# Longer row-half stretches in a fused attention and token-mixing kernel

## The chip, the cores and the metric

The kernel runs on one core of a Trainium2 chip. The metric is the device time of the program in microseconds, the median of several runs.

## The reference

The output mixes an attention with a token-mixing MLP through a sigmoid gate per token, in float32. Sizes: 2048 tokens (S), width 640 (D), 32 query heads of width 20 that share one key and one value head, hidden width 1728 (F).

```python
g = sigmoid((x * gate_w).sum(-1, keepdims=True))
# attention
q = (x @ wq) -> (32 heads, S, 20);  k = x @ wk;  v = x @ wv
p = softmax(q @ k.T * 20 ** -0.5);  a = (p @ v, heads joined) @ wo
# MLP over the token axis
h = layernorm(x)
u = gelu(einsum("bsd,sf->bdf", h, w1) + b1)
b = transpose(einsum("bdf,fs->bds", u, w2) + b2)
out = g * a + (1 - g) * b
```

## The kernel before

Large products are kept accurate by splitting each float32 operand into a high and a low part (tiles named `hi` and `lo`) and adding three products. The order of the instructions on every engine is written out by hand; no scheduler moves them.

A first part makes the projections q, k, v, the layer norm h and the first 10 of the 28 tiles of the MLP's first product. What follows is the loop that the change is about. It goes through 512 **units**: 32 groups n (512 queries of four heads) times 16 key blocks kb of 128 keys. For each unit:

- four **score** matmuls `s` (`qk`, L632), each with 62 rows of contraction, so each uses only one half of TensorE's rows, half 0 or half 1 (two matmuls per half). Both halves can run at once. ScalarE turns each into a `p` tile by an exponential (L635).
- one **o visit** (`pv_mm`, L659): p times v, accumulated over the 16 key blocks. It uses all rows and a quarter of the columns for each of the four heads, so it cannot run beside the row-half work.
- two extra rows of the score contraction hold minus the row maximum, which a separate pass has to find beforehand: **max matmuls** `ms` (L466, 60 rows, also in row halves), each read by a VectorE reduction (L469) into a tile `mp`. 64 of them make the maxima of one group; `ms_done` then reduces them (mm, L480) and splits them on GpSimd (mn, L482 to L484). `store_max` transposes them on VectorE (mt, L490) and stores them to memory, and `fetch_max` (L498) brings them into the query tile `qst` of a later group. The max pass runs 48 matmuls per half ahead of the scores when the loop starts.

Into the row half that the scores leave idle goes other matrix work, in steps `g` of 64 rows by 320 columns: first the rest of the MLP's first product (**W1**, L867), then its second product (**W2**, L704), then the attention's **output product** (L816) for the first half of the tokens. The weights of W1 and W2 arrive in chunks: a load (L99, L105), then a split on GpSimd (L123, L124) in `w1_upto`. A g accumulator is one PSUM bank, which both row halves must not write at once; so whenever the half changes, VectorE writes a `flag` (L645) after the last g step of one half, and the first of the other half waits for it.

One **phase** k of the loop, with b = k % 2: half b runs the four score matmuls of units k-1 and k and three or four ms; the other half runs g steps and the rest of the ms; then unit k-1 gets its o visit. `beside` merges the two halves' lists into one program order by nominal costs (`X_US` 0.232 for s and ms, `F_US` 0.147 for g). The last 24 units (`stretch`, the **tail**) take two units together, with two o visits behind them. PSUM has eight banks: three for s, three for ms, one for g, one for o.

Behind group n's last visit o is transposed on VectorE (ot, L668), divided by the row sums on GpSimd, transposed back (on, L675) and split into oh and ol, which are stored (`later`, one step per phase through `settle`). The tanh chain of the gelu goes through `pop_chain`, one step per phase. All loads and stores are issued by SyncE's queue in program order.

Of the kernel before, what the change touches and what calls it, by code (L numbers as in the profile page):

```python
# [17 lines left out]
P = 128  # L18
S, D, H, DH, F = 2048, 640, 32, 20, 1728
NS = S // P  # L20
# [17 lines left out]
def mix_kernel(ctx: ExitStack, tc: tile.TileContext, A_x, A_wq, A_wk, A_wv, A_wo,  # L38
# [400 lines left out]
    u0 = upool.tile([P, 2 * FC * HD2], F32R, name="u0")  # L439
    u_hi = [view(t, 0, FC) for t in (u0, slot[0])]  # L440
    u_lo = [view(t, FC * HD2, FC) for t in (u0, slot[0])]
    pp_pool = ctx.enter_context(tc.tile_pool(name="pp", bufs=12))
    ev = ctx.enter_context(tc.tile_pool(name="ev", bufs=1))
    ps_m = ctx.enter_context(tc.tile_pool(name="ps_m", bufs=3, space=PSUM))
    ps_g = ctx.enter_context(tc.tile_pool(name="ps_g", bufs=1, space=PSUM))
    mpool = ctx.enter_context(tc.tile_pool(name="mpool", bufs=2))
    mmpool = ctx.enter_context(tc.tile_pool(name="mmpool", bufs=2))

    row_max = {}
    mtiles = {}  # L450
    given = [0, 0]
    issued = [0, 0]
# [23 lines left out]
    def ms_done():  # L476
        n = len(row_max)
        if n < NU and min(issued) >= 32 * (n + 1):
# [5 lines left out]
            nc.gpsimd.tensor_sub(mn[:, 1, :], mm, f32(mn[:, 0, :]))  # L484
            row_max[n] = mn

    def store_max(n):
        mn = row_max[n]
        mt = mpool.tile([P, 32], F32, name="mt")
        nc.vector.transpose(mt, f32(mn).rearrange("p j c -> p (j c)"))  # L490
        nc.sync.dma_start(out=m_scr[n], in_=mt)
# [110 lines left out]
    def second():  # L602
        right.close()
        pools["rows"] = ctx.enter_context(tc.tile_pool(name="rows", bufs=3, side="right"))

    wos = {}

# [45 lines left out]
    def pv_mm(u):  # L653
        n, kb = units[u]
        if kb == 0:
            otile[0] = ps_o.tile([P, NB], F32, name="o")
        o = otile[0]
        for hh in range(4):
            nc.tensor.matmul(o[32 * hh:32 * hh + 32, :], v_sb[:, kb, :], ptiles.pop((u, hh)),  # L659
                             start=(kb == 0), stop=(kb == NS - 1), skip_group_check=True)  # L660
        if kb == NS - 1:
            qb, g = divmod(n, NQ)
            ot = ev.tile([P, NB // 32, 32], F32, name="ot")
            rl = ev.tile([P, NB // 32], F32, name="rl")
            on = ev.tile([P, NB], F32, name="on")
            oh = ev.tile([P, NB], F32R, name="oh")
            ol = ev.tile([P, NB], F32R, name="ol")
            nc.vector.transpose(ot.rearrange("p c e -> p (c e)"), o)  # L668

            def scale():  # L670
                nc.vector.reciprocal(rl, ot[:, :, DH])
                (nc.vector if spare[0] else nc.gpsimd).tensor_mul(ot, ot, rl[:, :, None].to_broadcast([P, NB // 32, 32]))

            def back():
                nc.vector.transpose(on, ot.rearrange("p c e -> p (c e)"))  # L675

            def high():
                osplit[:] = [oh, ol]
                if n < NU - 1:
                    nc.gpsimd.tensor_copy(oh, on)  # L680
                else:
                    nc.scalar.activation(oh, on, AF.Copy)

            def low():
                (nc.vector if n == NU - 1 else nc.gpsimd).tensor_sub(ol, on, f32(oh))
                for j, t in enumerate((oh, ol) if n < NU - 1 else ()):
                    for hh in range(4):
                        r = (4 * g + hh) * DH
                        nc.sync.dma_start(out=o_scr[j, r:r + DH, qb * NB:(qb + 1) * NB],
                                          in_=f32(t[32 * hh:32 * hh + DH, :]))  # L690

            later.extend((None, scale, back, high, low))

    def b2_jobs(st):
        hold = {}

        def mm(fc, k, d, half):
            if not hold.get("n"):
                hold["p"], hold["n"] = ps_g.tile([P, NB], F32, name="g"), 0
            wh, wl = w1t[W2 + 4 * st + fc // HS]  # L700
            w, u = ((wh, u_hi), (wh, u_lo), (wl, u_hi))[k]
            hold["n"] += 1
            r = slice(64 * half, 64 * half + 64)
            other_tile(half, nc.tensor.matmul(hold["p"][:, :HD2], w[r, fc % HS, :], u[d][r, fc, :],  # L704
                             start=(hold["n"] == 1), stop=(hold["n"] == 6 * FC - 3)))
# [10 lines left out]

        def steps(d):
            full = [[(fc, k), (fc, k)] for fc in range(FC - 1) for k in range(3)]
            return [[lambda fc=fc, k=k, h=h: mm(fc, k, d, h) for h, (fc, k) in enumerate(f)]
                    for f in full + [[(FC - 1, 0), (FC - 1, 1)], [(FC - 1, 2)]]]  # L720

        return (lambda: None), [(steps(d), lambda d=d: done(d)) for d in range(2)]

# [129 lines left out]
    def b1_jobs(d, fc):  # L853
# [16 lines left out]
        def done():  # L870
            gelu(d, fc, [hold["p"]])

        return load, [([[lambda h=h, st=st, k=k: mm(st, k, h) for h in range(2)]
                        for st in range(NS) for k in range(3)], done)]

    def batches(tiles, counts):
# [10 lines left out]
                    out.append(([r[c[j]:c[j + 1]] for r, c in zip(rows, cut)], rest, [done] if j == cnt - 1 else []))  # L887
        return out

    k_tail = len(units) - TAIL  # L890
    todo = [divmod(i, FC) for i in range(PRO, 2 * FC)]
    seq = batches([b1_jobs(*t) for t in todo], [5] * len(todo))
    for i, (steps, rest, done) in enumerate(seq):
        item, j = divmod(i + 1, 5)
        rest.insert(0, lambda c=4 * (PRO + item) + (48 * j // 5) // 12: w1_upto(c + 4))
    b2 = [b2_jobs(st) for st in range(NS)]
    m = len(seq)
    seq += batches(b2, [4] * 2 * NS)
    for st in range(NS - 1):
        for j, n in ((1, 1), (2, 2), (3, 4)):  # L900
            seq[m + 8 * st + 4 + j][1].append(lambda c=W2 + 4 * (st + 1) + n: w1_upto(c))
    seq[-1][1].append(second)
    for c in range(DC):
        seq[m + 9 + 8 * c][1].append(lambda c=c: load_wo(c))
        seq[m + 11 + 8 * c][1].append(lambda c=c: split_wo(c))
    aj = [a_jobs(st) for st in range(NS - 8)]
    seq[-8][1].append(aj[0][0])
    twice = k_tail // 2 - len(seq) - 2 * len(aj)
    seq += batches(aj, [2 if i < twice else 1 for i in range(2 * len(aj))])
    ph = [(rows[1 - b], rest if b else [], done if b else []) for rows, rest, done in seq for b in range(2)]  # L910
    assert len(ph) == k_tail
    for i, k in enumerate((443, 451, 459, 467, 473, 477, 481, 485)):
        ph[k][1].append(lambda i=i: tail_load(i))

    X_US, F_US = 0.232, 0.147

    def beside(rows0, rows64, x):
        lanes = [list(rows0), list(rows64)]
# [20 lines left out]
        if not (r0 and st in held):  # L939
            tail_job(i)  # L940
    w1_upto(4 * PRO + 4)
    def settle(k):
        for _ in range(2 if spare[0] else 1):
            f = later.pop(0) if later else None
            if f:
                f()
        pop_chain()

    def visit(u):
        pv_mm(u)  # L950
        n, kb = units[u]
        if kb == 7 and n + 1 < NU:
            store_max(n + 1)
        if kb == 9 and n + 1 < NU:
            fetch_max(n + 1)

    for k in range(k_tail):
        b = k % 2
        ss = [lambda u=u, pr=pr: qk(u, pr, b) for u in (k - 1, k) for pr in range(2) if u >= 0]
        fs, rest, done = ph[k]  # L960
        ms = [[f for f in (ms_next(x) for _ in range(c)) if f] for x, c in (((b, 3), (1 - b, 1)) if len(fs) < 12 else ((b, 4), (1 - b, 0)))]
        lanes = [None, None]
        lanes[b] = lane_x(ss, ms[0])
        lanes[1 - b] = lane_f(ms[1], fs, done)
        if k == 0:
            (m0, m1, m2), (s0, s1) = ms[0], ss
            lanes[0] = [(3 * X_US, m0), (3 * X_US, m1), (X_US, s0), (X_US, m2), (X_US, s1)]
        beside(*lanes, b)
        ms_done()
        spare[0] = len(row_max) == NU  # L970
        settle(k)
        for f in rest:
            f()
        if k == k_tail - 4:
            raw = last_wo()
        if k == k_tail - 2:
            w_last = split_last(raw)
        if k:
            visit(k - 1)

    def stretch(k, n):
        lanes = [None, None]
        for b in range(2):
            own = [j for j in range(k, k + n) if j % 2 == b]
            ss = [lambda u=u, pr=pr, b=b: qk(u, pr, b) for j in own for u in (j - 1, j) for pr in range(2) if u < len(units)]
            fs = tail_take(b, math.ceil(len(tail[b]) * n / (len(units) + 1 - k)) + (n == 1) * (3 if not ss else -3))
            cut = [0] + [round(len(fs) * x) for x in ((0.25, 0.5, 0.75, 1.0) if n == 1 else
                                                          (0.18, 0.53, 0.82, 1.0) if b == k % 2 else (0.41, 0.71, 1.0, 1.0))]
            lanes[b] = [x for i in range(4) for x in [(X_US, y) for y in ss[i:i + 1]] +
                        [(F_US, f) for f in fs[cut[i]:cut[i + 1]]]]  # L990
        beside(*lanes, None)
        for j in range(k, k + n):
            settle(j)
            if 13 <= j - k_tail < 17:
                tail_load(8 + j - k_tail - 13)
            visit(j - 1)

    stretch(k_tail, 1)
    for k in range(k_tail + 1, len(units), 2):
        stretch(k, 2)  # L1000
    accs = {}

    for c in range(CUT // P, DC):
# [57 lines left out]
```

## Time and profile before

| | us |
|---|---|
| median of three runs (1698.72 to 1698.84) | 1698.8 |
| the profiled execution, its span | 1697.4 |
| loop: first W1 step to the end of the last single visit | 179.4 to 1614.5 |
| busy in the span: PE, DVE, ACT, POOL | 1690.2, 1435.0, 1189.8, 570.4 |

The profile shows one execution. PE is the matrix engine, PEld its weight loads, DVE VectorE, ACT ScalarE, POOL GpSimd, SPq SyncE's queue of transfers. A row of the order of time has the start and the duration in us, the engine, the source line, the operation, output and input with their sizes, a count, and in brackets the idle time before it with what ended it. A row of a group has a count, busy time in us and the mean of one in ns. A row of the waits has the time in all, how many and the longest. Matmuls overlap, so a PE that is busy 100% is not a PE at its peak.

### The profile page before, as it was taken

What the parts mean: (1) busy time and instruction counts of PE and PEld (TensorE: products, weight loads), DVE (VectorE), ACT (ScalarE), POOL (GpSimd) and SP (SyncE); (2) the same over time, 40 slices, a digit from 0 to 9 for tenths busy, and PEclk for the clock granted to TensorE, in tenths of its full rate; (3) what the DMA queues carried; (4) which work ended last, traced back from release to release, by engine and by line L of the source; (5) the groups of instructions that cost most, each with busy time, mean ns of one, the idle gap of its engine ahead of it and who ended that gap; (6) DMA issues with size and microseconds to landing.
All of it is one profiled execution on the core that took longest, in us unless ns stands there. A gap on an engine that the chain in (4) does not pass through costs nothing.

```text
span 1697.4 us, 39056 instructions
## 1 busy us (share of the span) xinstructions
PE 1690.2 (100%) x14865; PEld 1103.0 (65%) x14865; DVE 1435.0 (85%) x2915; ACT 1189.8 (70%) x2322; POOL 570.4 (34%) x723
## 2 busy tenths in 40 slices
PE   9999999999999999999999999999999999999998
PEld 7899766666666666666666666666666666555666
DVE  6679898888888888888888888888888888888734
ACT  4445677777777777777777777777777777777775
POOL 6467644544445454322222212222221111111200
PEclk9999999999999999999999999999999999999999
DMA  7665322222222222121112222212111222344411
GB/s 212 192 177 147 94 64 69 65 64 64 60 69 70 70 70 69 50 64 52 57 49 70 70 60 62 63 56 61 52 52 35 62 63 64 92 113 144 132 57 57
DMA packets 173377, 135.45 MB, mean 80 GB/s; under 512 B 32729, under 2 KB 139382, under 8 KB 173190
## 3 DMA queue, kind: packets, MB, share of 16 engines
q1 hardware_dynamic: 172902, 132.63, 28.0%
q8 instruction: 117, 1.92, 0.5%
q14 instruction: 70, 0.57, 0.1%
q10 hardware_dynamic: 288, 0.33, 0.1%
HBM read 100.27 MB, written 31.65 MB: 78 GB/s over the span
## 4 chain that ended last, share of the span: by engine, by line
PE 96%; issue 2%; DVE 1%; SPq 1%; DMA 0%; POOL 0%; ACT 0%; POOLq 0%; DVEq 0%; ACTq 0%
PE o L659 30%; PE s L632 18%; PE ms L466 17%; PE g L704 12%; PE g L867 8%; PE pp L293 4%; PE pu L576 4%; PE g L816 2%; PE ms L773 1%; PE pt L285 0%; DVE mp L469 0%; PE g L773 0%; DVE st L226 0%; SPq L190 0%; SPq L188 0%
## 5 line engine op out<-in xcount | busy, mean ns | idle before, releaser
L469 DVE TENSOR_REDUCE mp<-ms 128x1 f32<-128x512 f32 x2048 | 1278.4, 684 | 171.1 <-PE ms L466 164.5
L635 ACT ACTIVATE p<-s 128x512 f32<-128x512 f32 x2048 | 1069.1, 603 | 397.4 <-PE s L632 393.8
L466 PE MATMUL ms<-kst,qmx 60*128 60x512 f32 x2048 | 846.8, 421 | 0.9 <-DVE mp L469 0.7
L632 PE MATMUL s<-qst,kst 62*128 62x512 f32 x2048 | 745.1, 404 | 0.0
L659 PE MATMUL o<-p,v_sb 128*32 128x512 f32 x4096 | 554.7, 604 | 0.0
L466 PEld LDWEIGHTS ms<-kst,qmx 60*128 60x128 f32 x2048 | 378.3, 185 | 213.6 <-DVE flag L645 181.1
L632 PEld LDWEIGHTS s<-qst,kst 62*128 62x128 f32 x2048 | 378.2, 186 | 11.5 <-issue 10.9
L867 PE MATMUL g<-slot,wh 64*128 64x320 f32 x1152 | 281.4, 318 | 0.0
L124 POOL TENSOR_TENSOR wl<-wr,wh 128x512 fp32r<-128x512 f32 (+1 forms) x176 | 219.9, 1251 | 35.8 <-ACT wh L121 21.3
L867 PEld LDWEIGHTS g<-slot,wh 64*128 64x128 f32 x1152 | 190.6, 184 | 59.8 <-DVE flag L645 59.8
L123 POOL CAST wh<-wr 128x512 fp32r<-128x512 f32 (+1 forms) x136 | 79.8, 587 | 444.4 <-PE g L704 281.7
L704 PE MATMUL g<-slot,wh 64*128 64x320 f32 x864 | 208.9, 317 | 0.0
L704 PE MATMUL g<-u,wh 64*128 64x320 f32 x864 | 208.8, 317 | 0.0
L659 PEld LDWEIGHTS o<-p,v_sb 128*32 128x32 f32 x4096 | 93.6, 108 | 137.7 <-issue 130.4
L867 PE MATMUL g<-slot,wl 64*128 64x320 f32 x576 | 179.4, 311 | 0.0
L704 PEld LDWEIGHTS g<-slot,wh 64*128 64x128 f32 x864 | 142.3, 184 | 40.2 <-DVE flag L645 40.2
L704 PEld LDWEIGHTS g<-u,wh 64*128 64x128 f32 x864 | 142.3, 184 | 40.2 <-DVE flag L645 40.2
L704 PE MATMUL g<-slot,wl 64*128 64x320 f32 x432 | 135.0, 313 | 0.0
L704 PE MATMUL g<-u,wl 64*128 64x320 f32 x432 | 134.9, 313 | 0.0
L867 PEld LDWEIGHTS g<-slot,wl 64*128 64x128 f32 x576 | 106.1, 184 | 15.1 <-DVE flag L645 15.1
L704 PEld LDWEIGHTS g<-slot,wl 64*128 64x128 f32 x432 | 79.6, 184 | 13.4 <-DVE flag L645 13.4
L704 PEld LDWEIGHTS g<-u,wl 64*128 64x128 f32 x432 | 79.5, 184 | 13.4 <-DVE flag L645 13.4
(195 smaller groups left out, 1404.0 us busy)
## 6 DMA issues: line engine op xcount, KB each, us to landing
wr<-in_B_w_dram SPq DMA_DIRECT2D x152, 256.0 KB
qmx<-q_scr SPq DMA_DIRECT2D x192, 80.0 KB
qst<-q_scr SPq DMA_DIRECT2D x192, 80.0 KB
y_scr<-yo SPq DMA_DIRECT2D x16, 320.0 KB
slot<-o_scr SPq DMA_DIRECT2D x16, 320.0 KB
o_scr<-oh SPq DMA_DIRECT2D x124, 40.0 KB
o_scr<-ol SPq DMA_DIRECT2D x124, 40.0 KB
q_scr<-qh SPq DMA_DIRECT2D x19, 256.0 KB
```

Source lines behind the costliest of these rows:

```text
L123: nc.gpsimd.tensor_copy(wh, wr)
L124: nc.gpsimd.tensor_sub(wl, wr, f32(wh))
L293: nc.tensor.matmul(pp, w, t, start=first and n == 0, stop=not more and n == len(steps) - 1)
L466: nc.tensor.matmul(ms, qmax[n][64 * b:64 * b + 60, pr, qt * P:(qt + 1) * P], kst[64 * b:64 * b + 60, kq * NB:(kq + 1) * NB], start=True, s ...
L469: nc.vector.tensor_reduce(mtiles[n][:, c, kq:kq + 1], ms, axis=AX.X, op=ALU.max)
L576: nc.tensor.matmul(pu[r][:, :HD2], w[rows, c, :], h[rows, st, :], start=(st == 0 and k == 0), stop=(st == NS - 1 and k == 2))
L632: nc.tensor.matmul(s, kst[64 * b:64 * b + 62, kb * P:(kb + 1) * P], q[64 * b:64 * b + 62, pr, :], start=True, stop=True)
L635: nc.scalar.activation(p, s, AF.Exp, scale=SCALE)
L659: nc.tensor.matmul(o[32 * hh:32 * hh + 32, :], v_sb[:, kb, :], ptiles.pop((u, hh)), start=(kb == 0), stop=(kb == NS - 1), skip_group_check ...
L704: other_tile(half, nc.tensor.matmul(hold["p"][:, :HD2], w[r, fc % HS, :], u[d][r, fc, :], start=(hold["n"] == 1), stop=(hold["n"] == 6 * F ...
L816: other_tile(half, nc.tensor.matmul(hold["p"][:, :HD2], o[r, c, :], w[r, c, d * HD2:(d + 1) * HD2], start=(hold["n"] == 1), stop=(hold["n" ...
L867: other_tile(half, nc.tensor.matmul(hold["p"][:, :HD2], w[r, st % HS, :], h[d][r, st, :], start=(hold["n"] == 1), stop=(hold["n"] == 6 * NS)))
```

## The change

The loop takes four units at a time. A **stretch** j, with h = j % 2 and i = j // 2, runs all eight score matmuls of units 4i to 4i+3 that belong to half h; g steps run in the other half; behind it stand the o visits of units 2j-2 and 2j-1. There are 244 stretches in place of 488 phases. W1 tiles are cut into two pieces of two stretches (24 g steps a half), in place of five pieces of two phases; W2 as before per unit, 20 or 21 steps a stretch; the output product gets more stretches, 44. The max matmuls are no longer three plus one per phase: each stretch gets a part that is proportional to a nominal length (`took`), and they are dealt to the two halves so that both lists are nominally equally long. `p` gets 16 buffers in place of 12; oh and ol take the places of ot and on (but for the last group). Row maxima are stored right behind the stretch in which they are complete (`store_maxima`), and fetched after visit 11 in place of 9. Weight chunks are split behind the stretch that uses the chunk last whose buffer they take. `settle` runs once and `pop_chain` twice a stretch. The tail is twelve stretches of two units, and the last two visits follow it.

```diff
-    pp_pool = ctx.enter_context(tc.tile_pool(name="pp", bufs=12))
+    pp_pool = ctx.enter_context(tc.tile_pool(name="pp", bufs=16))
...
+    def store_maxima():
+        while len(stored) < len(row_max):
+            store_max(len(stored))
...
-            oh = ev.tile([P, NB], F32R, name="oh")
-            ol = ev.tile([P, NB], F32R, name="ol")
+            if n < NU - 1:
+                oh, ol = ot.rearrange("p c e -> p (c e)").bitcast(F32R), on.bitcast(F32R)
+            else:
+                oh, ol = (pools["last"].tile([P, NB], F32R, name=name) for name in ("oh", "ol"))
...
-    seq = batches([b1_jobs(*t) for t in todo], [5] * len(todo))
-    for i, (steps, rest, done) in enumerate(seq):
-        item, j = divmod(i + 1, 5)
-        rest.insert(0, lambda c=4 * (PRO + item) + (48 * j // 5) // 12: w1_upto(c + 4))
-    b2 = [b2_jobs(st) for st in range(NS)]
+    seq = batches([b1_jobs(*t) for t in todo], [2] * len(todo))
     m = len(seq)
-    seq += batches(b2, [4] * 2 * NS)
+    seq += batches([b2_jobs(st) for st in range(NS)], [2] * 2 * NS)
...
+    for c in range(4 * PRO + 4, len(chunks)):
+        ph[last_use[c - 4]][1].append(lambda c=c: w1_upto(c + 1))
...
     X_US, F_US = 0.232, 0.147
+    took = [max(2 * 8 * X_US + len(fs) * F_US + 2 * 2.05, 2 * 4.9) for fs, _, _ in ph]
+    share = [sum(took[:j]) / sum(took) for j in range(n_st + 1)]
...
-        if kb == 7 and n + 1 < NU:
-            store_max(n + 1)
-        if kb == 9 and n + 1 < NU:
+        if kb == 11 and n + 1 < NU:
             fetch_max(n + 1)
...
-    for k in range(k_tail):
-        b = k % 2
-        ss = [lambda u=u, pr=pr: qk(u, pr, b) for u in (k - 1, k) for pr in range(2) if u >= 0]
-        fs, rest, done = ph[k]
-        ms = [[f for f in (ms_next(x) for _ in range(c)) if f] for x, c in (((b, 3), (1 - b, 1)) if len(fs) < 12 else ((b, 4), (1 - b, 0)))]
+    for j in range(n_st):
+        h, i = j % 2, j // 2
+        ss = [lambda u=u, pr=pr: qk(u, pr, h) for u in range(4 * i, 4 * i + 4) for pr in range(2)]
+        fs, rest, done = ph[j]
+        to = 64 * NU - sum(given) if j == n_st - 1 else round((32 * NU * 2 - LEAD * 2) * share[j + 1]) - given_to
+        given_to += to
+        own = round((to + F_US / X_US * len(fs) - len(ss)) / 2)
+        if h:
+            own = (given[0] - given[1] + to + 1) // 2
+        own = min(to, max(0, own))
+        ms = [[f for f in (ms_next(x) for _ in range(c)) if f] for x, c in ((h, own), (1 - h, to - own))]
         lanes = [None, None]
-        lanes[b] = lane_x(ss, ms[0])
-        lanes[1 - b] = lane_f(ms[1], fs, done)
+        lanes[h] = lane_x(ss, ms[0])
+        lanes[1 - h] = lane_f(ms[1], fs, done)
+        pop_chain()
+        beside(*lanes, h)
         ms_done()
         spare[0] = len(row_max) == NU
-        settle(k)
+        settle()
+        pop_chain()
         for f in rest:
             f()
+        store_maxima()
...
-        if k:
-            visit(k - 1)
+        if j:
+            visit(2 * j - 2)
+            visit(2 * j - 1)
```

More of the change, by code (lines that the diff above doesn't have):

```diff
@@ L447, in mix_kernel @@
     mmpool = ctx.enter_context(tc.tile_pool(name="mmpool", bufs=2))
-    row_max = {}
+    row_max, stored = {}, []
     mtiles = {}
@@ L485, in ms_done @@
             row_max[n] = mn
+    def store_maxima():
+        while len(stored) < len(row_max):
+            store_max(len(stored))
     def store_max(n):
         mn = row_max[n]
+        stored.append(n)
         mt = mpool.tile([P, 32], F32, name="mt")
@@ L604, in second @@
         pools["rows"] = ctx.enter_context(tc.tile_pool(name="rows", bufs=3, side="right"))
+        pools["last"] = ctx.enter_context(tc.tile_pool(name="last", bufs=1, side="right"))
     wos = {}
@@ L692, in pv_mm, with of_chunk @@
             later.extend((None, scale, back, high, low))
+    def of_chunk(c, f):
+        f.chunk = c
+        return f
     def b2_jobs(st):
@@ L718, in steps @@
             full = [[(fc, k), (fc, k)] for fc in range(FC - 1) for k in range(3)]
-            return [[lambda fc=fc, k=k, h=h: mm(fc, k, d, h) for h, (fc, k) in enumerate(f)]
-                    for f in full + [[(FC - 1, 0), (FC - 1, 1)], [(FC - 1, 2)]]]
+            return [[of_chunk(W2 + 4 * st + fc // HS, lambda fc=fc, k=k, h=h: mm(fc, k, d, h))
+                     for h, (fc, k) in enumerate(f)] for f in full + [[(FC - 1, 0), (FC - 1, 1)], [(FC - 1, 2)]]]
         return (lambda: None), [(steps(d), lambda d=d: done(d)) for d in range(2)]
@@ L871, in done @@
             gelu(d, fc, [hold["p"]])
-        return load, [([[lambda h=h, st=st, k=k: mm(st, k, h) for h in range(2)]
+        return load, [([[of_chunk(base + st // HS, lambda h=h, st=st, k=k: mm(st, k, h)) for h in range(2)]
                         for st in range(NS) for k in range(3)], done)]
@@ L888, in batches @@
         return out
-    k_tail = len(units) - TAIL
+    n_st = (len(units) - TAIL) // 2
     todo = [divmod(i, FC) for i in range(PRO, 2 * FC)]
-    seq = batches([b1_jobs(*t) for t in todo], [5] * len(todo))
-    for i, (steps, rest, done) in enumerate(seq):
-        item, j = divmod(i + 1, 5)
-        rest.insert(0, lambda c=4 * (PRO + item) + (48 * j // 5) // 12: w1_upto(c + 4))
-    b2 = [b2_jobs(st) for st in range(NS)]
+    seq = batches([b1_jobs(*t) for t in todo], [2] * len(todo))
     m = len(seq)
-    seq += batches(b2, [4] * 2 * NS)
-    for st in range(NS - 1):
-        for j, n in ((1, 1), (2, 2), (3, 4)):
-            seq[m + 8 * st + 4 + j][1].append(lambda c=W2 + 4 * (st + 1) + n: w1_upto(c))
+    seq += batches([b2_jobs(st) for st in range(NS)], [2] * 2 * NS)
     seq[-1][1].append(second)
     for c in range(DC):
-        seq[m + 9 + 8 * c][1].append(lambda c=c: load_wo(c))
-        seq[m + 11 + 8 * c][1].append(lambda c=c: split_wo(c))
+        seq[m + 4 * c + 4][1].append(lambda c=c: load_wo(c))
+        seq[m + 4 * c + 5][1].append(lambda c=c: split_wo(c))
     aj = [a_jobs(st) for st in range(NS - 8)]
-    seq[-8][1].append(aj[0][0])
-    twice = k_tail // 2 - len(seq) - 2 * len(aj)
+    seq[-4][1].append(aj[0][0])
+    twice = n_st // 2 - len(seq) - 2 * len(aj)
     seq += batches(aj, [2 if i < twice else 1 for i in range(2 * len(aj))])
     ph = [(rows[1 - b], rest if b else [], done if b else []) for rows, rest, done in seq for b in range(2)]
-    assert len(ph) == k_tail
-    for i, k in enumerate((443, 451, 459, 467, 473, 477, 481, 485)):
-        ph[k][1].append(lambda i=i: tail_load(i))
+    assert len(ph) == n_st
+    last_use = {}
+    for i, (fs, _, _) in enumerate(ph):
+        for f in fs:
+            c = getattr(f, "chunk", None)
+            if c is not None:
+                last_use[c] = i
+    for c in range(4 * PRO + 4, len(chunks)):
+        ph[last_use[c - 4]][1].append(lambda c=c: w1_upto(c + 1))
+    for i, j in enumerate((221, 225, 229, 233, 238, 239, 241, 242)):
+        ph[j][1].append(lambda i=i: tail_load(i))
     X_US, F_US = 0.232, 0.147
+    took = [max(2 * 8 * X_US + len(fs) * F_US + 2 * 2.05, 2 * 4.9) for fs, _, _ in ph]
+    share = [sum(took[:j]) / sum(took) for j in range(n_st + 1)]
     def beside(rows0, rows64, x):
@@ L941, in mix_kernel, with settle @@
     w1_upto(4 * PRO + 4)
-    def settle(k):
+    def settle():
         for _ in range(2 if spare[0] else 1):
@@ L946, in settle @@
                 f()
-        pop_chain()
     def visit(u):
@@ L951, in visit @@
         n, kb = units[u]
-        if kb == 7 and n + 1 < NU:
-            store_max(n + 1)
-        if kb == 9 and n + 1 < NU:
+        if kb == 11 and n + 1 < NU:
             fetch_max(n + 1)
-    for k in range(k_tail):
-        b = k % 2
-        ss = [lambda u=u, pr=pr: qk(u, pr, b) for u in (k - 1, k) for pr in range(2) if u >= 0]
-        fs, rest, done = ph[k]
-        ms = [[f for f in (ms_next(x) for _ in range(c)) if f] for x, c in (((b, 3), (1 - b, 1)) if len(fs) < 12 else ((b, 4), (1 - b, 0)))]
-        lanes = [None, None]
-        lanes[b] = lane_x(ss, ms[0])
-        lanes[1 - b] = lane_f(ms[1], fs, done)
[L965 to L968, printed above, removed]
+    given_to = 0
@@ L969, in mix_kernel @@
         ms_done()
         spare[0] = len(row_max) == NU
-        settle(k)
+        settle()
+        pop_chain()
         for f in rest:
             f()
-        if k == k_tail - 4:
+        store_maxima()
+        if j == n_st - 3:
             raw = last_wo()
-        if k == k_tail - 2:
+        if j == n_st - 1:
             w_last = split_last(raw)
-        if k:
-            visit(k - 1)
-    def stretch(k, n):
+        if j:
+            visit(2 * j - 2)
+            visit(2 * j - 1)
@@ L982, in stretch @@
+    def stretch(i):
+        u0 = 2 * n_st + 2 * i
         lanes = [None, None]
         for b in range(2):
[L984 to L988, printed above, removed]
@@ L989, in stretch @@
-            lanes[b] = [x for i in range(4) for x in [(X_US, y) for y in ss[i:i + 1]] +
-                        [(F_US, f) for f in fs[cut[i]:cut[i + 1]]]]
-        beside(*lanes, None)
[L992 to L1000, printed above, removed]
+            ss = [lambda u=u, pr=pr, b=b: qk(u, pr, b) for u in (u0, u0 + 1) for pr in range(2)]
@@ new lines, in stretch @@
+            fs = tail_take(b, math.ceil(len(tail[b]) / (TAIL // 2 - i)))
+            cut = [0] + [round(len(fs) * x) for x in ((0.18, 0.53, 0.82, 1.0) if b else (0.41, 0.71, 1.0, 1.0))]
+            lanes[b] = [x for n in range(4) for x in [(X_US, ss[n])] + [(F_US, f) for f in fs[cut[n]:cut[n + 1]]]]
+        beside(*lanes, None)
+        settle()
+        settle()
+        pop_chain()
+        if i in (7, 8):
+            tail_load(2 * i - 6)
+            tail_load(2 * i - 5)
+        visit(u0 - 2)
@@ L1001, in mix_kernel @@
+        visit(u0 - 1)
+    for i in range(TAIL // 2):
+        stretch(i)
+    visit(len(units) - 2)
+    visit(len(units) - 1)
     accs = {}
```

## The prediction

> **What bounds the kernel now.** I read the page's span, the busy times and the chain that ended last, then busy times by stretch for the loop, then the order of time in single phases.
>
> ```profile
> span 1697.4 us, 39056 instructions
> PE 1690.2 (100%) x14865; PEld 1103.0 (65%) x14865; DVE 1435.0 (85%) x2915; ACT 1189.8 (70%) x2322; POOL 570.4 (34%) x723
> PE 96%; issue 2%; DVE 1%; SPq 1%; DMA 0%; POOL 0%; ACT 0%; POOLq 0%; DVEq 0%; ACTq 0%
> 179.40:1614.50 1435.10, 1434.91 (x12601) 890.55 (x12599) 1268.06 (x2592) 1055.75 (x2055) 447.69 (x593) 1.00 0.25 69
> ```
>
> The chain is 96% TensorE. The last line is the loop (columns: stretch, its length, busy time of PE, PEld, DVE, ACT, POOL, then granted clock 1.00, DMA share, GB/s). It holds 488 phases, 2.94 us each; DVE is busy 1268 of 1435 us, close behind PE. How far behind matters here, so two phases in order of time (start, duration, then the operation); the first fence is from the W2 product, the second from W1:
>
> ```profile
> 931.69 1.10 PE L659 MATMUL o<-p,v_sb 128*32 128x512 f32 x8
> 932.72 0.50 PE L466 MATMUL ms<-kst,qmx 60*128 60x512 f32 x1
> 933.26 2.50 DVE L469 TENSOR_REDUCE mp<-ms 128x1 f32<-128x512 f32 x4 [0.24 <-PE ms L466]
> 933.49 2.06 ACT L635 ACTIVATE p<-s 128x512 f32<-128x512 f32 x4 [0.81 <-PE s L632]
> 934.30 0.40 PE L466 MATMUL ms<-kst,qmx 60*128 60x512 f32 x1
> 934.63 1.06 PE L659 MATMUL o<-p,v_sb 128*32 128x512 f32 x8
> ```
>
> ```profile
> 400.66 0.50 PE L466 MATMUL ms<-kst,qmx 60*128 60x512 f32 x1
> 401.47 0.39 PE L632 MATMUL s<-qst,kst 62*128 62x512 f32 x1
> 401.94 0.39 PE L632 MATMUL s<-qst,kst 62*128 62x512 f32 x1
> 402.57 1.06 PE L659 MATMUL o<-p,v_sb 128*32 128x512 f32 x8
> 405.47 1.11 PE L659 MATMUL o<-p,v_sb 128*32 128x512 f32 x8
> ```
>
> A phase is row-half matmuls, then one o visit. From o to o it takes 934.63-931.69 = 2.94 us in W2 and 2.90 in W1, so two phases are 5.88 and 5.80. Score and max matmuls of a row half start .235 us apart (401.47 to 401.94 holds two). DVE begins .54 after the first ms. Four reductions take 2.50; with the page's mean of one,
>
> ```profile
> L469 DVE TENSOR_REDUCE mp<-ms 128x1 f32<-128x512 f32 x2048 | 1278.4, 684 | 171.1 <-PE ms L466 164.5
> L635 ACT ACTIVATE p<-s 128x512 f32<-128x512 f32 x2048 | 1069.1, 603 | 397.4 <-PE s L632 393.8
> ```
>
> they end one every (2.50-.684)/3 = .605 us; exponentials likewise one every (2.06-.603)/3 = .486. With four ms in a phase and three ms buffers only the fourth ms needs a buffer back: at .54+.684 = 1.22 us, when it comes at 1.58 anyway (934.30-932.72). Nothing stalls, PE sets the pace. Near the loop's end one phase shows the other regime:
>
> ```profile
> 1458.77 0.50 PE L466 MATMUL ms<-kst,qmx 60*128 60x512 f32 x1
> 1459.31 2.50 DVE L469 TENSOR_REDUCE mp<-ms 128x1 f32<-128x512 f32 x4 [0.45 <-PE ms L466]
> 1460.05 0.18 PEld L466 LDWEIGHTS ms<-kst,qmx 60*128 60x128 f32 x1 [0.26 <-DVE mp L469]
> 1460.06 0.73 PE L632 MATMUL s<-qst,kst 62*128 62x512 f32 x2
> 1460.72 1.07 PE L659 MATMUL o<-p,v_sb 128*32 128x512 f32 x8
> ```
>
> Here the fourth ms comes early and is held until the first reduction ends (1459.31+.684 = 1459.99) plus .06. An s goes with it in the other half, a second s follows, and o begins .66 after the release. PE stops for a held ms: its queue is in order, so the g, s and o matmuls of both halves stand behind it, and ACT behind them.
>
> **The change, part by part.** *Switches.* 488 phases become 244 stretches (the built program has 244 flags and 16 o matmuls, two visits, behind each stretch). The tail already runs two visits together:
>
> ```profile
> 1632.47 0.40 PE L632 MATMUL s<-qst,kst 62*128 62x512 f32 x1
> 1632.80 1.92 PE L659 MATMUL o<-p,v_sb 128*32 128x512 f32 x16
> 1634.65 0.50 PE L632 MATMUL s<-qst,kst 62*128 62x512 f32 x2
> ```
>
> The last row-half matmul starts .33 before o, and a double visit takes 1.85 until the next row-half matmul; a single one takes 1.03 (931.69 to 932.72). By PE alone a W1 stretch (8 s and 8 ms in one half, 24 g in the other) has its sixteenth matmul at .81+12x.235 = 3.63 and lasts 3.63+.33+1.85 = 5.81, with 24 pieces of g where two old phases held about 19. A W2 stretch has its last at about 3.2 and lasts 5.38 instead of 5.88. That is the gain on offer.
>
> The Trainium skill, TensorEngine Tiling (Array Packing), Key Properties, says that changing the tiling mode drains the array. The .33 us ahead of each o agrees; halving the switches is by that rule a gain, which the next step takes away.
>
> *The burst.* A stretch now carries 7, 8 or 9 ms (built order: W1 43 stretches with 8 and 29 with 9; W2 128 with 8; the output product 29 with 7 and 15 with 8), still on three buffers. Reduction k ends at .54+.684+.605(k-1) after the first ms, and ms k+3 waits for it, plus .05. So ms 7 starts no earlier than .54+2.50+.05 = 3.09, ms 8 at 3.70, ms 9 at 4.30. PE wants ms 8 at about 3.2 to 3.4: it stands about .3 to .5 us in every stretch, and DVE has nothing left during the end of the next visits (its eighth reduction ends at .54+2.50+4x.605 = 5.46), so it can't work ahead.
> - W2: ms 8 and the last s go together at 3.70; 3.70+.33+1.85 = 5.88, x128 = 753 us.
> - W1 with 8: one s follows the held ms, o starts .66 after it as at 1460.06; 6.21, x43 = 267. With 9: 4.30+.33+1.85 = 6.48, x29 = 188.
> - Output product with short lists (24 stretches): with 7, the eighth s waits for the fifth exponential, .77+2.06+.486+.05 = 3.37 (.77 is 933.49-932.72), so 5.55, x18 = 100; with 8, 5.88, x6 = 35. Long lists (20): 5.55 x11 = 61, and 8 between 5.88 and 6.21, 6.05 x9 = 54.
>
> Sum 1458, less 1.85 as the first stretch has no visit: 1456. Against the loop's 1435 this is +21.
>
> The same page, Performance Considerations, PSUM Bottleneck, warns that tiling speeds up the array and not the reading of its results. By that rule these stretches are reduction-paced, as here; no number of the sum rests on it.
>
> *Row maxima (store_maxima).* Before, the transpose mt came several phases after the maximum mm; now it stands right behind it on DVE and waits for three POOL operations, and, in about 25 of 30 units of 16 key blocks, the o transpose stands behind mt.
>
> ```profile
> 762.51 0.22 DVE L480 TENSOR_REDUCE mm<-mp 128x16 f32<-128x64 f32 x1
> 762.82 0.25 POOL L482 TENSOR_SCALAR mm<-mm 128x16 f32<-128x16 f32 x1 [8.76 <-DVE mm L480]
> 763.42 0.22 POOL L484 TENSOR_TENSOR mn<-mm,mn 128x16 fp32r<-128x16 f32 x1
> 765.34 0.20 DVE L490 STREAM_TRANSPOSE mt<-mn 128x32 f32<-128x32 f32 x1
> 788.91 0.72 DVE L668 STREAM_TRANSPOSE ot<-o 128x512 f32<-128x512 f32 x1
> ```
>
> From mm to POOL's end 763.64-762.51 = 1.13, with mt and hand-offs about 1.43. Reductions end at 5.46, mt at 6.89, ot some .64 later, at 7.53; the next stretch's first reduction would begin at 5.88+.54 = 6.42. All reductions of the next stretch are 1.1 late, and its ms 8 with them. 25x1.1 + 5x.57 (mm alone .47, ot alone .1) = 30 us. Bounds: 0, if the next stretch had slack, which the held ms 8 excludes mostly; and 30x3, if POOL is in the middle of a split of 1.84 (below). I take 30.
>
> *Queues.* fetch_max now runs after visit 11 instead of 9, and weight chunks are split two or three at once behind a stretch.
>
> ```profile
> L498 SPq DMA_DIRECT2D qst<-m_scr x128: 638/639/1056, 169.3 to 1619.7; - x128
> SPq L498 <- DMA m_scr<-mt: 37.2, 29, 2.9
> L124 POOL TENSOR_TENSOR wl<-wr,wh 128x512 fp32r<-128x512 f32 (+1 forms) x176 | 219.9, 1251 | 35.8 <-ACT wh L121 21.3
> L123 POOL CAST wh<-wr 128x512 fp32r<-128x512 f32 (+1 forms) x136 | 79.8, 587 | 444.4 <-PE g L704 281.7
> ```
>
> From the end of stretch 8n+6 to the scores that need the fetch there are two double visits and one stretch, 1.85+4.0+1.85 = 7.7 us; four issues of .64 and a landing (2.9 is the longest wait for a small transfer that the second row shows) make 5.5. A split takes .59+1.25 = 1.84; the first piece of a new chunk is wanted 12 g pieces into the next W2 stretch, 1.85+1.7 = 3.6 after. Both cost nothing; if SP is still held by a weight load, each us late costs 30. The 16 p buffers equal what is alive at most (8 waiting, 8 new), and in-order visits free them before they are asked for. oh and ol in the places of ot and on: their stores go out three stretches ahead of the next ot; nothing. The tail keeps its pairs: 0, less than a us.
>
> **Sum.** Loop 1456+30 = 1486 against 1435: +51. The profiled execution has 1697.4, the median of the runs 1698.8, so 1.4 lies around the span. 1697.4+51+1.4 = 1750.
>
> **The rivals.**
> - *PE sets the pace after all (faster).* If the held ms cost nothing: 72x5.81 + 128x5.38 + 24x4.4 + 20x5.1 = 1315, +30 for the maxima: 1343 with the first visit off, -92, so 1607. For it: PE is 100% busy and saves 244 switches. Against it: 1460.05 shows the hold, and every stretch with 8 has it. It decides where the reductions end .48 apart instead of .605 (fifth one half a us earlier).
> - *Only the buffer limit counts.* The extra .33 behind ms 8 in W1 and the 30 us are hidden: 43x5.88+188+753+250-2 = 1442, +7: 1706.
> - *POOL is late for the maxima.* mt waits behind one split each time: 30x1.84 = 55 more, 1805. Against it: POOL was busy 448 of 1435 us.
> - *The clock.* The granted clock was 1.00 in the loop. At .9 the 2.2 us of a stretch that PE still paces grow by .24, x244 = 60: 1810. The Trainium skill, TensorE: Matmul & The Clock Gate, A second HAM failure mode, reports that small idle gaps between groups of matmuls made the clock oscillate; no row of this kernel shows it.
>
> **How the numbers follow.** Forecast .71 (its own range 1720 to 1785: maxima 0 to 60, the .33 each way), PE pace .09, buffer limit only .08, POOL late .10, clock .02. The range 1695 to 1806 leaves out the first rival and little else. Beyond .2% (3.4 us, about what runs within .1 us of each other and a changed layout can tell apart): slower .87, same .03, faster .10.
>
> **What would show it.** The wait that should grow has this row now:
>
> ```profile
> PEld ms L466 <- DVE mp L469: 30.6, 53, 0.8
> ```
>
> Right: ms waiting for mp in almost every loop stretch (53 times and 30.6 us now, then some 200 times and 80 to 120 us), two-visit periods of 5.9 in W2 and 6.2 to 6.5 in W1, DVE busy share of the loop lower than before's 88%, double visits at 1.85, and mt waiting for mn about 1 us some 30 times. Wrong: W2 periods near 5.4 (the reductions keep up), PE waiting for chunks from POOL or for qst's DMA, or a granted clock under 1.00.

## The result and the profile after

The changed kernel takes 1754.78 us (median, 1754.69 to 1755.05) against 1698.82: a ratio of 1.033, 95% interval 1.031 to 1.034. It is slower by 3.3%. The forecast was 1750.

The page of the changed kernel has these lines in the places of those shown of the kernel before: the span, the busy times, the engines of the chain that ended last and its lines; then the busy times of the loop, which now ends 1.85 us after the start of its last o visit at 1668.95.

```profile
span 1752.6 us, 38439 instructions
PE 1723.7 (98%) x14865; PEld 1118.9 (64%) x14865; DVE 1411.5 (81%) x2671; ACT 1188.5 (68%) x2322; POOL 572.5 (33%) x723
PE 68%; DVE 26%; issue 3%; SPq 1%; ACT 0%; POOL 0%; DMA 0%; POOLq 0%; DVEq 0%; ACTq 0%
PE o L665 25%; DVE mp L469 25%; PE ms L466 15%; PE s L638 9%; PE g L879 4%; PE pp L293 4%; PE pu L581 4%; PE g L716 4%; PE g L828 1%; PE ms L785 1%; DVE ot L676 1%; ACT p L641 0%; PE pt L285 0%; PE g L785 0%; SPq L190 0%
179.40:1670.80 1491.40, 1469.24 (x12590) 907.71 (x12589) 1245.01 (x2348) 1055.39 (x2057) 446.11 (x590) 1.00 0.24 66
```

The chain was 96% TensorE; now a quarter of it runs through the max reductions of L469. The loop grew from 1435.1 to 1491.4 us, +56.3; what follows it shrank from 82.9 to 81.8. That is the whole difference of the spans, 1752.6-1697.4 = 55.2. DVE has the same 1952 reductions in the loop but is busy 1245 of 1491 us, 83% instead of 88%: VectorE stands in the chain and is idle more. The granted clock stayed at 1.00.

One ordinary W2 stretch of the changed kernel in order of time, without the g steps and most of the s:

```profile
744.79 1.92 PE L665 MATMUL o<-p,v_sb 128*32 128x512 f32 x16
746.64 0.18 PEld L466 LDWEIGHTS ms<-kst,qmx 60*128 60x128 f32 x1 [0.84 <-DVE mp L469]
746.64 0.50 PE L466 MATMUL ms<-kst,qmx 60*128 60x512 f32 x1
747.18 4.29 DVE L469 TENSOR_REDUCE mp<-ms 128x1 f32<-128x512 f32 x7 [1.06 <-PE ms L466]
747.41 4.07 ACT L641 ACTIVATE p<-s 128x512 f32<-128x512 f32 x8 [1.88 <-PE s L638]
749.82 1.00 PE L466 MATMUL ms<-kst,qmx 60*128 60x512 f32 x2
750.31 0.18 PEld L466 LDWEIGHTS ms<-kst,qmx 60*128 60x128 f32 x1 [0.41 <-DVE mp L469]
750.32 0.50 PE L638 MATMUL s<-qst,kst 62*128 62x512 f32 x1
750.75 1.49 PE L665 MATMUL o<-p,v_sb 128*32 128x512 f32 x12
751.38 0.68 DVE L469 TENSOR_REDUCE mp<-ms 128x1 f32<-128x512 f32 x1
```

(The last row of o counts 12 of 16 because the view ends inside the visit.) The first reduction begins .54 after the first ms. The eighth ms has its weights loaded at 750.31, 3.67 us after the first ms, released by the fifth reduction, which ends about .04 before; the last score goes with it at 750.32 and o follows .43 later. DVE's eighth reduction ends at 752.06. From there to the next stretch's first ms DVE has no reduction to do; the 1.06 in the brackets is the same gap one stretch earlier. From o to o it is 750.75-744.79 = 5.96 us, where two phases of the kernel before took 5.88.

The waits of the changed kernel (waiting engine and line, what released it, us in all, times, longest):

```profile
PEld ms L466 <- DVE mp L469: 174.8, 389, 0.8
PEld s L638 <- ACT p L641: 32.5, 116, 0.8
DVE mt L495 <- POOL mn L484: 25.5, 31, 1.0
```

The first had 30.6 us in 53 waits before. It is not all held ms. Taken one by one, 90 of its 389 waits (75.5 us) are the .84 that PEld stands idle at the end of a visit, as at 746.64. That .84 stands behind every visit of both kernels, under the name of whatever was released last. What is left, 299 waits and 99.4 us, are ms held inside a stretch; in the kernel before it was 26 waits and 8.0 us.

Where the maxima of a group are complete and its o transpose (ot) falls behind the same stretch, the next is longer (6.77 from o to o). That is so 16 times in W2:

```profile
834.95 1.92 PE L665 MATMUL o<-p,v_sb 128*32 128x512 f32 x16
836.19 0.21 DVE L480 TENSOR_REDUCE mm<-mp 128x16 f32<-128x64 f32 x1
836.80 0.50 PE L466 MATMUL ms<-kst,qmx 60*128 60x512 f32 x1
837.35 0.21 DVE L495 STREAM_TRANSPOSE mt<-mn 128x32 f32<-128x32 f32 x1 [0.95 <-POOL mn L484]
837.55 0.72 DVE L676 STREAM_TRANSPOSE ot<-o 128x512 f32<-128x512 f32 x1
838.20 4.26 DVE L469 TENSOR_REDUCE mp<-ms 128x1 f32<-128x512 f32 x7
```

The stretch starts at 836.80 and its reductions could start at 837.34; mt waits .95 for POOL, ot stands behind it, and the first reduction begins at 838.20, .86 late. In W1 the two fall into different stretches. One with ot alone:

```profile
336.06 1.92 PE L665 MATMUL o<-p,v_sb 128*32 128x512 f32 x16
337.92 0.49 PE L466 MATMUL ms<-kst,qmx 60*128 60x512 f32 x1
338.11 0.72 DVE L676 STREAM_TRANSPOSE ot<-o 128x512 f32<-128x512 f32 x1 [0.96 <-POOL yo L540]
338.75 4.84 DVE L469 TENSOR_REDUCE mp<-ms 128x1 f32<-128x512 f32 x8
342.86 1.06 PE L665 MATMUL o<-p,v_sb 128*32 128x512 f32 x8
```

From o to o it takes 6.80, the others like it 6.81 or 6.82, in place of 6.55; maxima without ot make a W1 stretch 0 to .12 longer.

### The profile page after: what moved, and what is told of

Read it like the earlier page. It is cut to its first block, busy times and chain, and to the rows that moved or that the text cites. A ratio compares the mean times of both kernels' runs of the same rounds, so it can differ in the third digit from the quotient of the medians.

```text
span 1752.6 us, 38439 instructions
## 1 busy us (share of the span) xinstructions
PE 1723.7 (98%) x14865; PEld 1118.9 (64%) x14865; DVE 1411.5 (81%) x2671; ACT 1188.5 (68%) x2322; POOL 572.5 (33%) x723
## 4 chain that ended last, share of the span: by engine, by line
PE 68%; DVE 26%; issue 3%; SPq 1%; ACT 0%; POOL 0%; DMA 0%; POOLq 0%; DVEq 0%; ACTq 0%
PE o L665 25%; DVE mp L469 25%; PE ms L466 15%; PE s L638 9%; PE g L879 4%; PE pp L293 4%; PE pu L581 4%; PE g L716 4%; PE g L828 1%; PE ms L785 1%; DVE ot L676 1%; ACT p L641 0%; PE pt L285 0%; PE g L785 0%; SPq L190 0%
## 5 line engine op out<-in xcount | busy, mean ns | idle before, releaser
L469 DVE TENSOR_REDUCE mp<-ms 128x1 f32<-128x512 f32 x2048 | 1253.5, 680 | 216.5 <-PE ms L466 192.2
L466 PE MATMUL ms<-kst,qmx 60*128 60x512 f32 x2048 | 892.8, 443 | 20.4 <-DVE mp L469 6.3
L638 PE MATMUL s<-qst,kst 62*128 62x512 f32 x2048 | 804.4, 410 | 1.1 <-DVE yo L517 0.8
L466 PEld LDWEIGHTS ms<-kst,qmx 60*128 60x128 f32 x2048 | 375.8, 184 | 236.8 <-DVE mp L469 174.8
L665 PE MATMUL o<-p,v_sb 128*32 128x512 f32 x4096 | 492.3, 598 | 0.0
L638 PEld LDWEIGHTS s<-qst,kst 62*128 62x128 f32 x2048 | 378.5, 186 | 45.3 <-ACT p L641 32.5
L665 PEld LDWEIGHTS o<-p,v_sb 128*32 128x32 f32 x4096 | 106.9, 109 | 220.8 <-issue 218.5
L879 PEld LDWEIGHTS g<-slot,wh 64*128 64x128 f32 x1152 | 194.3, 184 | 30.9 <-DVE flag L651 14.9
L716 PEld LDWEIGHTS g<-slot,wh 64*128 64x128 f32 x864 | 143.0, 184 | 13.4 <-DVE mp L469 13.4
L680 POOL TENSOR_TENSOR ot<-ot,rl 128x512 f32<-128x512 f32 x30 | 31.5, 1049 | 240.7 <-DVE rl L679 219.6
L879 PEld LDWEIGHTS g<-slot,wl 64*128 64x128 f32 x576 | 106.3, 185 | 0.0
```

What stands on the lines that cost most here:

```text
L466: nc.tensor.matmul(ms, qmax[n][64 * b:64 * b + 60, pr, qt * P:(qt + 1) * P], kst[64 * b:64 * b + 60, kq * NB:(kq + 1) * NB], start=True, s ...
L469: nc.vector.tensor_reduce(mtiles[n][:, c, kq:kq + 1], ms, axis=AX.X, op=ALU.max)
L638: nc.tensor.matmul(s, kst[64 * b:64 * b + 62, kb * P:(kb + 1) * P], q[64 * b:64 * b + 62, pr, :], start=True, stop=True)
L879: other_tile(half, nc.tensor.matmul(hold["p"][:, :HD2], w[r, st % HS, :], h[d][r, st, :], start=(hold["n"] == 1), stop=(hold["n"] == 6 * NS)))
```

## The experiments

The theory: three ms buffers and one reduction every .605 us hold the eighth ms of a burst, PE's in-order queue stands, and DVE idles later because it can't get ahead. The main rivals: DVE's work as a whole sets the pace; the longer stretch costs PE time by itself; the inline store of the maxima does it.

**Shorter reductions.** Four kernels read fewer columns of each ms tile, so that keys are left out of the row maxima: three from the changed kernel (256, 384 and 448 of 512 columns), one from the kernel before (256).

```diff
-            nc.vector.tensor_reduce(mtiles[n][:, c, kq:kq + 1], ms, axis=AX.X, op=ALU.max)
+            nc.vector.tensor_reduce(mtiles[n][:, c, kq:kq + 1], ms[:, :256], axis=AX.X, op=ALU.max)
```

> The changed kernel, but each of the 2048 max reductions reads 256 of the 512 columns of its ms tile (half of the keys are left out of the row maxima; the other half of the reduction's time with it). Theory (three ms buffers and reductions .605 us apart hold ms 8): the hold goes, the eighth score (fifth exponential, 3.37 us) is next, so W2 periods fall from 5.95 to about 5.6, W1 to 5.85, the maxima stretches lose most of their .8; the loop falls from 1491 to about 1385, the time to about 1645. Rival (the longer stretch itself, its double visits or half switches, costs PE the time): periods stay above 5.8 and the time above 1720.

> The kernel before with the same half-width reductions (half of the keys left out of the row maxima). Theory: its phases are paced by PE, with the fourth ms late by nothing, so 1690 to 1699. Rival (reductions pace the kernel before as well): it falls as much as the changed one does, to below 1650. The difference to the run with the changed kernel at the same width is what the switches are worth when the reductions allow it: about 45 to 50 by theory.

> The changed kernel with reductions over 448 of 512 columns (an eighth of the keys left out of the row maxima). Theory: reductions end about .53 apart, ms 8 may go at 3.32, just under the eighth score's 3.37; W2 periods about 5.6, W1 5.85 with 8 ms and 6.15 with 9, time about 1680. Rival (DVE's total work, not the hold of the eighth ms, sets the pace): the time falls in proportion to the reductions, by an eighth of 1253 us or 157, to about 1600, or, if only PE counts, not at all.

> The changed kernel with reductions over 384 of 512 columns (a quarter of the keys left out of the row maxima). Theory: ms 8 may go at about 2.95, well under the eighth score, so a further cut brings nothing: within 8 us of the run with 256 columns (1661), against 1684 at 448 and 1755 at 512, a knee at reductions about .5 apart. Rival (DVE's work as a whole paces the loop): halfway between 1684 at 448 and 1661 at 256 minus what is left, so on a straight line from 1755 at 512 through 1684 at 448, near 1612.

| columns | changed kernel, us | kernel before, us | W1 from o to o | W2 from o to o |
|---|---|---|---|---|
| 512 | 1754.8 | 1698.8 | 6.18 and 6.55 | 5.96 |
| 448 | 1683.6 (.990, .988 to .992) | | 5.85 and 6.15 | 5.65 to 5.73 |
| 384 | 1663.2 (.979, .977 to .981) | | 5.78 to 5.81 | 5.65 to 5.72 |
| 256 | 1661.3 (ratio .977, .975 to .979) | 1696.8 (.998, .997 to .999) | 5.78 to 5.81 | 5.65 to 5.72 |

(The last two columns are ordinary stretches. Those with maxima or ot can be longer: 14 of the 128 in W2 take 6.13 to 6.20 at 448 columns, three or four take 5.76 to 6.01 at 384 and 256; in W1 seven to nine take 6.02 to 6.06 at 384 and 256.) The reductions of the run with 448 columns as a group, and two waits of the run with 384:

```profile
L469 DVE TENSOR_REDUCE mp<-ms 128x1 f32<-128x448 f32 x2048 | 1118.3, 614 | 274.0 <-PE ms L466 250.1 <-PE g L828 12.8 <-PE g L716 4.9
```

```profile
PEld s L638 <- ACT p L641: 47.4, 181, 0.8
PEld ms L466 <- DVE mp L469: 3.1, 12, 0.4
```

A W2 stretch of the run with 256 columns:

```profile
711.40 0.50 PE L466 MATMUL ms<-kst,qmx 60*128 60x512 f32 x1
712.23 4.03 ACT L641 ACTIVATE p<-s 128x512 f32<-128x512 f32 x8 [1.23 <-PE s L638]
714.84 0.50 PE L638 MATMUL s<-qst,kst 62*128 62x512 f32 x1
715.26 1.07 PE L665 MATMUL o<-p,v_sb 128*32 128x512 f32 x8
```

An eighth less of the reduction (614 ns in place of 680) takes 71 us off the changed kernel, the second eighth 20 more, the next quarter 2. That is the knee of a hold, not a straight line of work: at 384 columns the ms wait for reductions 3.1 us in all, in place of the 99.4 of holds at 512, and scores that wait for exponentials are what is left. In the last view the eighth score goes at 714.84, 3.44 us after the first ms, when the fifth exponential has just ended (712.23+4x.486+.6 = 714.8). The kernel before gains only 3 us from the same cut (1699.7 in that session): reductions don't pace it. With 256 columns in both, the changed kernel is 1696.8-1661.3 = 35.5 us faster than the kernel before. So the change as a whole does pay once the reductions are out of the way, and the longer stretch as such is not what costs; which of its parts pays was not separated. 35.5 is less than the 45 to 50 expected, and 1661 is 16 over the 1645 expected, mostly as W2 came out at 5.65 to 5.72 and not 5.6.

The runs with 256 and 384 columns beat both kernels by 2%, the one with 448 the kernel before by 1%. They are no drop-in: the softmax doesn't depend on the shift, but a shift taken over a part of the keys no longer bounds the exponent.

**One ms buffer less.** A third ms buffer is written once before the loop and read once after it, so two are left.

```diff
+    kept = ps_m.tile([P, NB], F32, name="ms")
+    nc.tensor.matmul(kept, kst[:64, :P], kst[:64, :NB], start=True, stop=True)
     given_to = 0
     for j in range(n_st):
...
+    nc.vector.tensor_reduce(flag, kept[:1, :], axis=AX.X, op=ALU.max)
+
     def stretch(i):
```

> The changed kernel with one of the three ms buffers taken out of use for the length of the loop. Theory: ms 8 then waits for the sixth reduction, 4.30 instead of 3.70 (up to 4.5 if a hand-over of .5 shows between reductions): W2 periods 6.55 to 6.8 instead of 5.95, W1 6.8 to 7.1, output product with 7 ms 5.95 or more; time 1890 to 1930. Rival (DVE's work as a whole): unchanged, as DVE has the same work and is idle a fifth of the loop.

1934.3 us. A W2 stretch of it:

```profile
905.00 0.50 PE L466 MATMUL ms<-kst,qmx 60*128 60x512 f32 x1
909.00 0.93 PE L466 MATMUL ms<-kst,qmx 60*128 60x512 f32 x2
909.87 1.92 PE L665 MATMUL o<-p,v_sb 128*32 128x512 f32 x16
```

The seventh and eighth ms go only from 4.00 us on, o at 4.87, the period is 6.73 (6.55 to 6.8 expected), W1 6.96 with 8 ms as expected (6.8 to 7.1) and 7.41 with 9, which is over it. DVE has the same reductions to do and is busy 78% of this loop, so its work as a whole is not what paces: the buffers are. The total is 4 us over the expected range.

**One buffer moved from s to ms.** Four ms, two s.

```diff
-            ms = ps_m.tile([P, NB], F32, name="ms")
+            taken[0] += 1
+            ms = (extra[0] if extra and taken[0] % 4 == 0 else ps_m).tile([P, NB], F32, name="ms")
...
-    ps_s = ctx.enter_context(tc.tile_pool(name="ps_s", bufs=3, space=PSUM))
+    ps_s = ctx.enter_context(tc.tile_pool(name="ps_s", bufs=2, space=PSUM))
+    extra.append(ctx.enter_context(tc.tile_pool(name="ps_x", bufs=1, space=PSUM)))
```

> The changed kernel with one PSUM buffer moved from the scores to the max matmuls: four ms, two s. Theory: ms 8 then waits for the fourth reduction (3.09) and is free, but the eighth s waits for the sixth exponential, .77+2.06+2x.486+.05 = 3.85: W2 periods 6.1 instead of 5.95, W1 with 9 ms about 6.1 instead of 6.55, output product 6.05 instead of 5.65; the wait of ms for mp falls from 175 us to under 40 and that of s for p grows from 32 to over 100; time 1755 to 1770. Rival (DVE's work as a whole sets the pace): the time and the periods stay, and the ms still wait.

1885.5 us (ratio 1.110, 1.108 to 1.112): far over the 1755 to 1770 expected. Both waits, then a W2 stretch in order of time:

```profile
PEld s L641 <- ACT p L644: 248.8, 802, 0.7
PEld ms L468 <- DVE mp L471: 53.0, 64, 0.8
```

```profile
903.16 0.50 PE L468 MATMUL ms<-kst,qmx 60*128 60x512 f32 x1
903.93 4.64 ACT L644 ACTIVATE p<-s 128x512 f32<-128x512 f32 x8 [1.92 <-PE s L641]
907.44 0.50 PE L641 MATMUL s<-qst,kst 62*128 62x512 f32 x1
907.87 0.64 PE L668 MATMUL o<-p,v_sb 128*32 128x512 f32 x4
```

The ms are released, as the theory says: of their 53.0 us, 62 waits (52.0) are the .84 behind a visit, and two (1.0 us) are held ms. But the scores are held far more than expected. Eight exponentials take 4.64 us in place of 4.07: with two buffers the next score is not ready when an exponential ends, and they start .58 apart instead of .49. The eighth score goes at 4.28 and not 3.85, and every stretch lasts about 6.55 or more. The step that failed in this expectation was the exponentials' spacing, taken from a run with three buffers. So neither of the two splits of six buffers that were run (three and three, four ms and two s) frees the stretch.

**The store of the maxima one stretch later.**

```diff
         beside(*lanes, h)
+        store_maxima()
         ms_done()
...
         for f in rest:
             f()
-        store_maxima()
```

(and once after the loop)

> The changed kernel with the row maxima stored one stretch later, so that the transpose mt does not wait for POOL on DVE's queue. Theory: the 30 stretches of 6.77 (W2) and 6.81 (W1) fall to about 6.1 and 6.2 to 6.6, in all 15 to 22 us, to about 1735. Rival (the o transpose that stands there too costs it): less than 6 us.

1745.5 us, 9.3 less (ratio 1.0265, 1.025 to 1.028), between the 15 to 22 expected and the rival's 6. The 16 stretches of 6.77 in W2 became 6.22, more than the 6.1 expected; that is 9 us. The four of 6.81 in W1 stayed, as they are those of ot, and so did the .26 in W2 that ot costs. So the wait for POOL is real and a sixth of the loss, but the expectation had taken the stretches of ot for stretches of the maxima, and there the rival was right.

**Max matmuls dealt evenly; and both.**

```diff
-    share = [sum(took[:j]) / sum(took) for j in range(n_st + 1)]
+    share = [j / n_st for j in range(n_st + 1)]
```

> The changed kernel with the max matmuls dealt evenly over the stretches (8 each) instead of by the stretches' nominal lengths. Theory: W1 loses its 29 stretches of 6.55 (-.37 each, -11), the output product gains 29 with 8 in place of 7 (+.3 each, +9), so -6 to +3 us. Rival (dealing by length keeps stretches from stalling): slower by over 10.

> Max matmuls dealt evenly and the row maxima stored one stretch later, both of the small repairs at once. Theory: dealing evenly already moved mm away from the o transpose and left mt only 8 us of waiting, so the two don't add up: 2 to 6 us under dealing evenly alone (1747), 1741 to 1745, still slower than the kernel before by 2.5%. Rival (independent effects): 17 under the changed kernel, 1738 or less.

Evenly: 1747.1 us, 7.7 less, a little better than the -6 to +3 expected. W1 has 62 of its 70 stretches at 6.17 to 6.20 and eight with ot at 6.39 to 6.46; it takes 10 us less, and the output product, now with 8 ms in every stretch, 7 more. Another 5 come from W2, where dealing did not change the count of ms: the o transpose and the maxima fall behind different stretches now (one of 6.18 and one of 6.22 in eight, in place of one of 6.77). Both edits: 1742.0 us (ratio 1.025, 1.0235 to 1.027), as expected 5 under the even deal; they overlap. It is the best version here that keeps the whole row maximum, and still slower than the kernel before.

## Why the prediction was right

- *What bounds the kernel before.* Right: its time moved by 3 us when half of every reduction was taken away, so reductions don't, and its chain is 96% TensorE.
- *The burst.* Right, and it carries the result. The eighth ms was forecast at 3.70 us and came at 3.67; W1 was forecast at 6.21 and 6.48 and came at 6.18 and 6.55; W2 at 5.88 and came at 5.96. The mis-sized term is the end of the stretch: from the last start to o I took .33 from a tail row whose last matmul had not been held; behind a held one it is .43, where the weights of the held ms are loaded only at its release (750.31). Over 128 W2 stretches that is 10 us. The output product was forecast at about 250 us and took, from o to o, 258. About 3 of the 8 are the same .10 (29 stretches with 7 ms at 5.65 for 5.55), 2 to 3 are six stretches of 6.06 in which an activation of the product's own output stands among the exponentials, and the rest are transposes. The sign to look for was sized right only after the visits are taken out of it: 80 to 120 us were forecast, the row has 174.8, and the holds in it are 99.4, though in 299 waits and not some 200.
- *The maxima.* Right in kind, too large: W2 has 16 such stretches of +.82, 13 us, where I had 1.1 each. The chain on DVE began a little earlier than my 5.46 and the stretch it delays was itself .08 longer. The count was wrong too: ot stood behind mt in 17 of 30 units, not 25, and apart from each other the two were priced the wrong way round (maxima 0 to .12 and ot .26 in W1, for .47 and .1). Added up, these stretches cost about 18 us, an estimate from their lengths over those of ordinary ones, and not 30.
- *The queues.* Costed at nothing, which fits. The longest waits of the changed kernel show PE waiting for reductions, exponentials and flags, not for weight chunks or for the fetched maxima; the growth of the loop is accounted for without them: 445 us in 70 W1 periods (6.36 each, where 43x6.21 and 29x6.48 make 6.32), 775.5 in W2, 258 in the output product.
- *The sum.* Forecast +51 on the loop, measured +56: +10 from the held end in W2, about +6 in the output product without its transposes, about -12 from the maxima and transposes. Errors of 10 us and more cancelled, so that 1750 came so near to 1754.8 is partly luck; that the loop grew, and by which hold, is not.
- *The rivals.* PE setting the pace did not happen: W2 took 5.96, not 5.38. Its price was wrong as well: with the reductions out of the way the changed kernel reached 1661, not 1607, because the eighth score then waits for the fifth exponential (5.65 in place of my 5.38). The knee forecast at reductions .48 apart lies between 448 columns, where they come one every .53 us, and 384, where it is .47. That only the buffer limit counts would have W1 with 8 ms at 5.88; it was 6.18. That POOL is late would have mt wait for a split of 1.84 each time; its 31 waits are 25.5 us in all and 1.0 at most. The clock stayed at 1.00, so the oscillation that the Trainium skill (TensorE: Matmul & The Clock Gate, A second HAM failure mode) reports for small gaps did not appear here. The Trainium skill's warning in TensorEngine Tiling (Array Packing), PSUM Bottleneck, is that tiling speeds up the array but not the reading of results. The runs agree in so far as the reading is what holds a burst here (99.4 us of holds); the tiling itself was the same in all of them.

## What to carry to other kernels

Fewer switches mean longer bursts, and a burst is limited by how far the reader of PSUM falls behind in it: with b buffers, matmul k can't start before reduction k-b ends, however idle that engine is on average. Before merging stretches, write down that time for the last matmul of the burst next to the time at which PE wants it. A share of busy time well under 100% on the reading engine says nothing against it: here that share fell while the engine came to hold a quarter of the chain.

## What the runs showed of the hardware

A matmul that waits for a buffer has, in the rows read here, its weight load held too: the load starts at the release (750.31; of the changed kernel's holds of ms 99.4 us are on PEld and 6.3 on PE itself), and from there to the next operation of the other tiling it takes .43 us in place of .33. The end of a visit leaves PEld idle for .84 us (746.64), and a row of the waits can hold such gaps. With two buffers between TensorE and ScalarE exponentials come .58 us apart in place of .49, and the scores wait for them 248.8 us in place of 32.5. A reduction over PSUM of 512, 448, 384 and 256 columns takes 680, 614, 551 and 422 ns, about 1 ns a column and 165 ns besides.
